# A fused sliding-window attention and feed-forward kernel on one core: residue order 0,2,1,3, VectorE masks for batch 1, w_f copies mostly on ScalarE

## The chip, the core and the metric

The kernel runs on one core of a Trainium2 chip. A core has five engines with a queue each: TensorE (PE in the profile, its weight loads as PEld), VectorE (DVE), ScalarE (ACT), GpSimd (POOL) and SyncE (SP). An engine takes its instructions in the order in which the program holds them and waits on semaphores for the others. Here GpSimd issues the loads that change the type from float32 to bfloat16, SyncE issues the stores and the transposes that a DMA makes. The metric is the device time of one execution in microseconds (us).

## What is computed

For each of 8 batches and 8 heads, 576 positions of 64 numbers attend to earlier positions. Heads 0 to 3 see the last 32 positions; heads 4 to 7 see every fourth position of the last 128. The result, as 4608 tokens of 512 numbers, goes through a gated feed-forward part.

```python
rel = pos[:, None] - pos[None, :]
mask_plain = (rel >= 0) & (rel < 32)
mask_dil = (rel >= 0) & (rel < 128) & (rel % 4 == 0)
scores = np.where(masks, q @ k.T / 8, -1e9)
attn = softmax(scores) @ v
x = attn.transpose(0, 2, 1, 3).reshape(4608, 512)
out = ((x @ w1) * (x @ w2)) @ w3 @ w_out
```

The weights w1 and w2 are 512 by 1024, w3 is 1024 by 1024, w_out is 1024 by 512.

## The kernel before

The kernel multiplies w3 and w_out into one matrix w_f (1024 by 512) on the chip, once, so that a token needs three products: with w1, with w2, and with w_f.

The order of all work is made by a planner that runs while the program is built. Each piece of work is a task with an engine, a supposed duration, dependencies, a priority and a number of PSUM banks (there are eight). `Plan.run` (line 70) plays through a clock of its own, gives each free engine the ready task with the lowest priority number, and hands out banks. The tasks are then emitted in order of their planned starts. So a supposed duration, a rank or a lead changes nothing but the order of the instructions in the queues and the banks.

Attention works by batch. A batch has two halves of heads, u = 0 (plain) and u = 1 (dilated), and in each six blocks of 96 query positions; the dilated heads are sorted by residue of the position modulo 4, so that their window is a band as well. The steps of a batch are:

- load of q, k and v by rows (lines 225 and 234). For batch 0 the first halves of q and k come by SyncE in float32 and ScalarE rounds them (line 240).
- transposition of q, k and v into columns by VectorE: `turn`, lines 344 and 357. v of batches 0 and 1 goes back to rows by TensorE (line 366) and is copied to `vp` (lines 376 and 378). From batch 2 on v is loaded straight into place (lines 248 and 262) with a copy for the halo (line 269).
- scores on TensorE (line 408), a group of blocks at a time, in four banks; exponential on ScalarE (line 419).
- the mask. In batches 0 and 1 (`BIASED = 2`) a group has three blocks, and four products of the identity with a bias table (line 391) put -30000 into the bank before the scores. From batch 2 on a group has five blocks (`GRP`), which may cross batches, and VectorE multiplies the exponentials by 0 or 1 in two halves (line 427). The 0/1 table `mask` is made by GpSimd from the bias table in five operations (line 327).
- P·V on TensorE (line 444), four steps per batch; reciprocal and normalisation on VectorE (lines 455 and 467).
- turning back into columns `XT`: by TensorE (line 484) and a copy by ScalarE or VectorE (lines 492 and 494) in batches 0 and 1, by a DMA transpose that SyncE issues (line 497) from batch 2 on.

The feed-forward part works in units k of 288 tokens, two a batch. For each of eight slices f it makes two groups of four products (line 516, with w1 and with w2), copies the first (ScalarE, line 527) and multiplies it with the second into `gt` (VectorE, line 532). After that eight products with w_f (line 543) give 128 output tokens, copied by ScalarE (line 554) and stored by SyncE (line 565). w_f is made in eight steps: transposes of a slice of w3 (line 573), a copy (ScalarE, line 580), eight products with w_out (line 585) and a copy into `wf_sb` (VectorE, line 595). All 36 outputs need all eight.

At the start, GpSimd's queue holds, in this order: the other loads of batch 0, w1 and w2 by halves of 512 columns, w_out in two halves, six slices of w3, q, k and v of batch 1, two slices of w3, q and k of batch 2, the mask operations, and the loads of v for batch 2. TensorE begins with 12 products on zeros (line 604).

The scores of a batch are held back so that they come `LEAD` batches ahead of the feed-forward part of their batch:

```python
pair = int(16 * (b - LEAD) + 4 * i)
```

Of the kernel before, what the change touches and what calls it, by code (L numbers as in the profile page):

```python
# [10 lines left out]
P = 128  # L11
# [8 lines left out]
S = 576  # L20
# [6 lines left out]
UNIT = 288  # L27
RING = 1152
BIG = 30000.0
BIASED = 2  # L30
TURNED = 2
ORDER = (2, 3, 0, 1)
RANK = dict(E=1.5, VK=1, K=0.4, N=3, T=1.5, VT=0.2, S=0.3, V=0.1, X=0.4)
WARM = 12
W3_FIRST = 6
SHIFT = {}
ON_DVE = ("K0.0", "K0.2", "K0.3", "K1.2", "VK0.1.0", "VK1.0.1")
GRP = 5
WHOLE = ("qn", "kn")
TURN_LAT = 2700  # L40
LEAD = 1.4
# [13 lines left out]
class Plan:  # L55
# [14 lines left out]
    def run(self):  # L70
# [41 lines left out]
        while len(order) < n:  # L112
            progress = True
            while progress:
                progress = False
                for e in engines:
                    if free[e] > now:
                        continue
                    for r, t in sorted(waiting[e], key=lambda x: x[1].prio):
                        if r > now:  # L120
                            continue
                        at = place(t) if t.slot else 0
                        if at is not None:
                            break
                    else:
                        continue
                    waiting[e].remove((r, t))
                    t.start = now
                    if e == "DMA":
                        free[e] = now + t.dur[0]  # L130
                        dma = max(dma, now + t.dur[0]) + t.dur[1]
                        t.end = dma + 1900
                    else:
                        t.end = free[e] = now + t.dur
                        if t.lat == TURN_LAT and dma > now:
                            t.lat += 3300
                    if t.slot:
                        t.place = at
                        held[at : at + t.slot] = [t] * t.slot
                        if t.slot == 4:  # L140
                            kept = None
                    order.append(t)
                    for u in users[id(t)]:
                        left[id(u)] -= 1
                        if not left[id(u)]:
                            r = max(d.end + (0 if d.eng == u.eng else d.lat) for d in u.deps)
                            waiting[u.eng].append((r, u))
                    progress = True
            ahead = [f for f in free.values() if f > now]
            ahead += [r for e in engines for r, _ in waiting[e] if r > now]  # L150
            ahead += [x for x in map(freed, held) if x is not None and x > now]
            if not ahead:
                left = [t.name for t in self.tasks if t.end is None]
                raise RuntimeError(f"the plan does not end: {left[:20]}")
            now = min(ahead)
# [4 lines left out]
def kernel(  # L160
# [28 lines left out]
    w3_pool = ctx.enter_context(tc.tile_pool(name="w3", bufs=8))  # L189
# [63 lines left out]
    def load_v_dil(b, m):  # L253
        vp = vps[b % 2]
        r, mu = 2 * (m // 3), m % 3
        runs = {
            0: [(0, 96, r, 0)],
            1: [(0, 48, r, 96), (48, 48, r + 1, 0)],
            2: [(0, 96, r + 1, 48)],
        }[mu]  # L260
        for p0, n, res, t0 in runs:
            nc.gpsimd.dma_start(  # L262
                out=vp[32 + p0 : 32 + p0 + n, 4:8, m, 0:D],
                in_=v_rows(b, 4, 4 * t0 + res, [[4 * D, n], [S * D, 4], [1, D]]),
            )
# [5 lines left out]
    def load_w(dst, src, c):  # L271
        f = slice(512 * c, 512 * (c + 1))
        nc.gpsimd.dma_start(
            out=dst[:, :, f], in_=src[:, f].rearrange("(a p) f -> p a f", p=P)
        )
# [32 lines left out]
    def blocks():  # L308

        base = bias[:, 6, :]
        by_res = base.rearrange("p (t r) -> p r t", r=4)
        nc.scalar.copy(
            out=bias[:, 0:4, :].rearrange("p i (r t) -> p i r t", r=4),
            in_=by_res.unsqueeze(1).to_broadcast([P, 4, 4, 24]),
        )
        nc.scalar.copy(out=bias[:, 4, :], in_=base)
        nc.scalar.copy(out=bias[:, 5, 0 : QB // 2], in_=base[:, 0 : QB // 2])
# [17 lines left out]
    def turn(b, u, nm, part):  # L337

        src = qk[(nm, b)][:, u, :].bitcast(U32)
        dst, pad = {"qn": (qts, 0), "kn": (kts, PADK), "vn": (vts, PADK)}[nm]  # L340
        d = dst[b % len(dst)].rearrange("p u w c -> p u (w c)").bitcast(U32)[:, u, :]
        if part is None:
# [3 lines left out]
        n, first, odd = ((5, 0, 2 * RUN + 4), (4, 2 * RUN, 5 - 2 * RUN))[part]  # L346
        o = bass.AP(
            tensor=d.tensor,
            offset=d.offset + pad + first,
            ap=[d.ap[0], [1, n], [RUN, 2], [9, 16], [odd, 2]],  # L350
# [3 lines left out]
            offset=src.offset + part * 64,  # L354
            ap=[src.ap[0], [128, n], [32, 2], [1, 32]],
# [200 lines left out]

    def store(i):
        o_sb = held[("o", i)]
        c0, end = i * P, (i + 1) * P
        at = c0  # L560
        while at < end:
            n = min(end, (at // RUN + 1) * RUN) - at
            b, x = at // S, at % S
            row = b * S + 4 * (x % RUN) + x // RUN
            nc.sync.dma_start(
                out=out[row : row + 4 * (n - 1) + 1 : 4, :], in_=o_sb[at - c0 : at - c0 + n, :]
            )
            at += n
# [9 lines left out]
    def w3_keep(ft):  # L578
        w3T[ft] = wk_pool.tile([P, KFF, P], BF16, tag="w3T", bufs=2, name="w3T")
        nc.scalar.copy(out=w3T[ft], in_=held[("x3", ft)])  # L580
# [13 lines left out]
    def w3_done(ft):  # L594
        nc.vector.tensor_copy(out=wf_sb[:, ft, :], in_=held[("wf", ft)])
# [10 lines left out]
    def first_constants():  # L606
        nc.vector.memset(warm, 0.0)
        nc.vector.memset(bias, 0.0)
# [9 lines left out]
    c0 = add("const", "DVE", 2500, [], first_constants, 0)  # L618
    add("warm", "PE", 1840 + 216 * WARM, [c0], warm_up, 0)
# [29 lines left out]

    def loads_w12(c):  # L650
        return [
            load("LW", 800, 3300, [], lambda d=d, s=s: load_w(d, s, c))
# [3 lines left out]
    for i, nm in enumerate(WHOLE):  # L656
        t = add(f"LF{nm}", "SP", 100, [], lambda nm=nm: load_whole(nm, rows_of[nm], 0), -9 + i,
                lat=4100 + 1350 * i)
# [7 lines left out]
    idt = add("ident", "DMA", (600, 0), [], lambda: make_identity(nc, ident), 2.5, lat=-1900)  # L666
    bnd = add("band", "DMA", (700, 0), [c0], band, 2.6, lat=-1800)
    blk = add("blocks", "ACT", 1200, [bnd], blocks, 0, lat=100)
    blk = add("no halo", "DVE", 150, [blk], no_halo, 0, lat=80)
    mk = add("masks", "DMA", (2500, 0), [blk], masks_of_bias, 26.5, lat=-1800)  # L670
    lw12 = [loads_w12(0), loads_w12(1)]
    for c in range(2):
        lwo[c] = load(f"LWO{c}", 600, 3300, [], lambda c=c: load_wo(c))
    def loads_w3(fts):
        for ft in fts:
            lw3[ft] = load(f"LW3.{ft}", 550, 1400, [], lambda ft=ft: load_w3(ft))

    loads_w3(range(W3_FIRST))
    for nm in ("qn", "kn", "vn"):
        loads_rows(nm, 1)  # L680
    loads_w3(range(W3_FIRST, KFF))

    FUSED, w3m = [], []
    for ft in range(KFF):
        x = add(f"W3T{ft}", "PE", 510, [lw3[ft], idt], lambda f=ft: w3_back(f), 6, slot=1,
                after=[w3m[-2] if len(w3m) > 1 else None])
        y = add("W3C", "ACT", 1012, [x], lambda f=ft: w3_keep(f), -1, lat=100,
                after=[w3m[-2] if len(w3m) > 1 else None])
        z = add(f"W3M{ft}", "PE", 1728, [y, lwo[0], lwo[1]], lambda f=ft: w3_mul(f), 7, slot=1)
        w3m.append(z)  # L690
        FUSED.append(add("W3D", "DVE", 688, [z], lambda f=ft: w3_done(f), -1, lat=100))
# [5 lines left out]
    def turns(b, u, nm, pr):  # L697
        parts = (None,) if u == 0 and nm != "qn" else (0, 1)
        old = last_v.get((b - 1, u)) if nm == "vn" else last_s.get((b - 2, u))
        ts = [  # L700
            add(f"T{nm}{b}.{u}.{part or 0}", "DVE",
                1245 if part is None else 750 if part == 0 else 630, [L[(nm, b, u)], c0],
                lambda part=part: turn(b, u, nm, part), pr, lat=80, after=[old])
# [3 lines left out]
        return ts  # L707

    vals, T = {}, {}
    for b in range(B):  # L710
# [4 lines left out]
        for u in range(2):  # L715
            T[(b, u)] = [
                t for nm in ("kn", "qn") for t in turns(b, u, nm, 10 * b + RANK["T"])
            ]
        for u in range(2):
            if b >= 2:  # L720
                break
            tv = turns(b, u, "vn", 10 * b + RANK["T"])
            for half in range(2):
                x = add(f"VT{b}.{u}.{half}", "PE", 420, tv + [idt],
# [8 lines left out]
        if b >= 2:  # L733
            hal = add(f"HALO{b}", "DVE", 820, LV[b], lambda b=b: halo_v(b), 10 * b + 2, lat=80)
# [5 lines left out]
        def group(blocks, biased):  # L740
# [4 lines left out]
            need = [t for at in sorted({x[0:2] for x in blocks}) for t in T[at]]  # L745
# [33 lines left out]
        while steps < 4 * B:  # L779
# [27 lines left out]
            else:  # L807
                x = add("XD" + n, "SP", 100, ns, st.back_dma, 0, lat=TURN_LAT)
# [7 lines left out]
    def ups(k, f):  # L816
# [3 lines left out]
        wl = lw12[f // 4]  # L820
# [14 lines left out]
    def downs(i):  # L835
# [5 lines left out]
        Y[i] = y  # L841
        cy = add("CY", "ACT", 585, [y], lambda: copy_y(i), -1, lat=100,
# [5 lines left out]
    for k in range(2 * B):  # L848
        for f in range(KFF):
            ups(k, f)  # L850
            if f % 3 == 1 and done < n_y and (done + 1) * P <= k * UNIT:
                downs(done)
                done += 1
# [44 lines left out]
```

## Time and profile before

| | us |
|---|---|
| median of five runs (259.69 to 260.49) | 260.34 |
| the profiled execution's own time | 260.24 |
| span in its profile, first to last instruction | 258.5 |
| first up-projection product (line 516) starts | 21.26 |
| last product with w_f ends | 254.1 |

| group in the profile | count | mean ns | busy us |
|---|---|---|---|
| TensorE up-projections, line 516 | 1024 | 286 | 136.0 |
| TensorE products with w_f, line 543 | 259 recorded of 288 | 379 | 65.0 |
| TensorE bias products, line 391 | 32 | 325 | 6.2 |
| VectorE gates, line 532 | 128 | 455 | 57.9 |
| VectorE mask products of five blocks' halves, line 427 | 28 | 650 | 17.5 |
| VectorE copies of w_f, line 595 | 8 | 692 | 5.5 |
| ScalarE exponentials of three blocks, line 419 | 8 | 1129 | 8.8 |
| ScalarE exponentials of five blocks, line 419 | 14 | 1771 | 24.8 |
| ScalarE output copies, line 554 | 36 | 586 | 21.1 |
| GpSimd mask operations, line 327 | 5 | 937 (median) | 4.8 |
| DMA transposes, line 497 | 24 | 4.9 us to landing (median) | |

Matmuls overlap in their pipeline, so the mean of one is longer than the distance from one to the next. A row of the timeline gives the start, the busy time, the engine, the line, what it writes and reads, the shape, the count, and in brackets the idle time before it with what ended it. In a table of stretches each engine has its busy time and, in brackets, its instructions; then come the granted clock of TensorE (1.00 is full), the share of the DMA engines, and GB/s.

### The profile page before, as it was taken

What the parts mean: (1) busy time and instruction counts of PE and PEld (TensorE: products, weight loads), DVE (VectorE), ACT (ScalarE), POOL (GpSimd) and SP (SyncE); (2) the same over time, 40 slices, a digit from 0 to 9 for tenths busy, and PEclk for the clock granted to TensorE, in tenths of its full rate; (3) what the DMA queues carried; (4) which work ended last, traced back from release to release, by engine and by line L of the source; (5) the groups of instructions that cost most, each with busy time, mean ns of one, the idle gap of its engine ahead of it and who ended that gap; (6) DMA issues with size and microseconds to landing.
All of it is one profiled execution on the core that took longest, in us unless ns stands there. A gap on an engine that the chain in (4) does not pass through costs nothing.

```text
span 258.5 us, 6708 instructions
## 1 busy us (share of the span) xinstructions
PE 244.7 (95%) x2699; PEld 167.9 (65%) x2732; DVE 166.5 (64%) x338; ACT 123.1 (48%) x211; POOL 65.2 (25%) x101
## 2 busy tenths in 40 slices
PE   6489999999999999999999999999999999999993
PEld 2367775576577677676667766677766766777661
DVE  3976435979898898898858687666654653333220
ACT  4465464493826373453653535636355343333331
POOL 8612476356401728232033050300000000000000
PEclk9589999999999999999999999999999999999998
DMA  7999999999998999999963949652406162211113
GB/s 221 202 207 202 209 212 210 201 86 190 162 175 159 182 190 116 179 197 206 202 86 53 102 55 144 98 78 53 109 23 93 42 90 63 82 39 44 43 41 122
DMA packets 58030, 33.40 MB, mean 129 GB/s; under 512 B 44688, under 2 KB 47760, under 8 KB 58000
## 3 DMA queue, kind: packets, MB, share of 16 engines
q0 software_dynamic: 37488, 18.81, 56.4%
q1 hardware_dynamic: 20512, 14.16, 25.6%
q8 instruction: 21, 0.34, 0.5%
q14 instruction: 9, 0.07, 0.1%
HBM read 38.80 MB, written 9.44 MB: 187 GB/s over the span
## 4 chain that ended last, share of the span: by engine, by line
PE 91%; ACT 3%; DVE 2%; DMA 2%; issue 1%; ACTq 0%; DVEq 0%
PE ps L516 49%; PE ps L543 23%; PE ps L585 5%; PE ps L444 5%; PE ps L408 4%; ACT et L419 2%; PE ps L391 2%; DMA gt<-in_q_dram 2%; PE ps L573 1%; PE ps L366 1%; PE ps L484 1%; DVE qt L357 1%; DVE kt L344 0%; ACT qn L240 0%; DVE vt L344 0%
## 5 line engine op out<-in xcount | busy, mean ns | idle before, releaser
L516 PE MATMUL ps<-XT,w_sb 128*128 128x288 bf16 x1024 | 136.0, 286 | 0.3 <-DVE gt L532 0.2
L516 PEld LDWEIGHTS <-w_sb 128*128 128x128 bf16 x1024 | 97.7, 98 | 30.1 <-issue 0.6
L532 DVE TENSOR_TENSOR gt<-ps,asb 128x288 bf16<-128x288 f32 x128 | 57.9, 455 | 55.2 <-PE ps L516 53.5
L527 ACT CAST asb<-ps 128x288 bf16<-128x288 f32 x128 | 51.0, 399 | 60.5 <-PE ps L516 57.7
L543 PE MATMUL ps<-wf_sb,gt 128*128 128x512 bf16 x259 | 65.0, 379 | 1.5 <-issue 0.2
L554 ACT COPY osb<-ps 128x512 f32<-128x512 f32 x36 | 21.1, 586 | 52.5 <-PE ps L543 47.1
L543 PEld LDWEIGHTS <-gt 128*128 128x128 bf16 x288 | 28.0, 98 | 27.7
L262 POOL DMA_DIRECT2D vp<-in_v_dram x48 | 30.2, 636 | 48.9 <-PE ps L444 16.2
L419 ACT ACTIVATE et<-ps 128x1920 bf16<-128x1920 f32 (+2 forms) x23 | 34.4, 1506 | 6.1 <-PE ps L408 5.0
L467 DVE TENSOR_TENSOR xo<-ps,rcp 96x384 bf16<-96x384 f32 (+1 forms) x48 | 31.8, 678 | 0.6
L357 DVE STREAM_TRANSPOSE qt<-qn 128x320 uint32<-128x320 uint32 (+1 forms) x32 | 21.6, 674 | 3.4 <-ACT qn L240 3.2
L427 DVE TENSOR_TENSOR et<-et,mask 128x960 bf16<-128x960 bf16 (+1 forms) x30 | 18.1, 630 | 3.8 <-ACT et L419 3.6
L444 PEld LDWEIGHTS <-et 128*128 128x128 bf16 x384 | 14.2, 98 | 3.8 <-ACT et L419 1.3
L444 PE MATMUL ps<-vp,et 128*128 128x65 bf16 x384 | 15.3, 193 | 1.1 <-ACT et L419 1.0
L585 PE MATMUL ps<-wo_sb,w3T 128*128 128x512 bf16 x60 | 14.6, 379 | 0.2
L408 PEld LDWEIGHTS <-kt 32*128 32x128 bf16 x768 | 9.5, 95 | 6.1 <-issue 5.6
L357 DVE STREAM_TRANSPOSE kt<-kn 128x320 uint32<-128x320 uint32 (+1 forms) x16 | 10.9, 683 | 3.6 <-PE ps L408 3.5
L408 PE MATMUL ps<-qt,kt 32*128 32x96 bf16 x768 | 12.9, 206 | 0.0
L344 DVE STREAM_TRANSPOSE kt<-kn 128x576 uint32<-128x576 uint32 x8 | 10.0, 1250 | 2.0 <-PE ps L408 2.0
L580 ACT COPY w3T<-ps 128x1024 bf16<-128x1024 bf16 x8 | 8.1, 1013 | 4.8 <-PE ps L573 4.7
L455 DVE RECIPROCAL rcp<-ps 96x12 f32<-96x12 f32 x32 | 6.5, 214 | 5.3 <-PE ps L444 5.1
L248 POOL DMA_DIRECT2D vp<-in_v_dram x6 | 7.3, 1209 | 10.5 <-PE ps L444 10.3
(49 smaller groups left out, 105.0 us busy)
## 6 DMA issues: line engine op xcount, KB each, us to landing
qn<-in_q_dram POOLq DMA_DIRECT2D x7, 576.0 KB, 7.5
kn<-in_k_dram POOLq DMA_DIRECT2D x7, 576.0 KB, 8.5
w_sb<-in_moe_w_dram POOLq DMA_DIRECT2D x4, 512.0 KB, 12.6
w3n<-in_moe_w_dram POOLq DMA_DIRECT2D x8, 256.0 KB, 15.2
out_dram<-osb SPq DMA_DIRECT2D x8, 256.0 KB, 2.9
out_dram<-osb SPq DMA_DIRECT2D x8, 224.0 KB, 2.9
vp<-in_v_dram POOLq DMA_DIRECT2D x6, 288.0 KB, 10.2
out_dram<-osb SPq DMA_DIRECT2D x8, 192.0 KB, 2.4
```

The source lines that it names most:

```text
L262: nc.gpsimd.dma_start(out=vp[32 + p0 : 32 + p0 + n, 4:8, m, 0:D], in_=v_rows(b, 4, 4 * t0 + res, [[4 * D, n], [S * D, 4], [1, D]]),)
L357: nc.vector.transpose(out=o, in_=i)
L408: nc.tensor.matmul(out=self.sp[:, g, QB * i : QB * i + QB], lhsT=kt[prt, u, QB * m : QB * m + P, c], rhs=qq, start=(c == 0 and not biased) ...
L419: nc.scalar.activation(out=ev, in_=self.sp[:, :, 0:x], func=ACT.Exp, scale=scale)
L444: nc.tensor.matmul(out=self.o[:, g, mm, :], lhsT=grp.et[:, c0 : c0 + P], rhs=vps[self.b % 2][:, 4 * self.u + g, 3 * self.hf + mm, 0 : D + ...
L467: nc.vector.tensor_tensor(out=dst, in0=self.o[0:QB, hs, :, 0:D], in1=self.rcp[0:QB, hs, :].unsqueeze(3).to_broadcast([QB, n, 3, D]), op=AL ...
L516: nc.tensor.matmul(out=o, lhsT=w_sb[:, c, f * P : (f + 1) * P], rhs=unit_cols(k, c), start=(j == 0), stop=(j == DCH - 1),)
L527: nc.scalar.copy(out=a_sb, in_=held[("a", k, f)])
L532: nc.vector.tensor_tensor(out=gt[:, f, c0 : c0 + UNIT].rearrange("p (r m t) -> p m r t", r=2, m=BLK), in0=held[("b", k, f)].rearrange("p ( ...
L543: nc.tensor.matmul(out=y, lhsT=gt[:, f, c0 : c0 + P], rhs=wf_sb[:, f, :], start=(f == 0), stop=(f == KFF - 1),)
L554: nc.scalar.copy(out=o_sb, in_=held[("y", i)])
L585: nc.tensor.matmul(out=o, lhsT=w3T[ft][:, g, :], rhs=wo_sb[:, g, :], start=(g == 0), stop=(g == KFF - 1),)
```

## The change

Parts of it:

- `RES = (0, 2, 1, 3)`: the dilated heads' residues are kept in this order, so that the first three blocks need residues 0 and 2 only. Addresses in `turn`, `load_v_dil`, `store` and the bias table follow. In batch 0, `turn` makes the second half of heads (u = 1) in four parts instead of two, and scores and v's transposes wait only for the parts that their half needs.
- `BIASED = 1`: batch 1's scores are grouped by five with batch 2's and masked by VectorE.
- Three of the eight copies into `wf_sb` stay on VectorE (slices 2, 5 and 7), five go to ScalarE. The `ON_DVE` list of other copies changes as well.
- The first loads have another order: k of batch 1, the first quarter of w1 and of w2, a slice of w3, their second quarters, their second halves, q and v of batch 1, w_out, six slices of w3; after the masks and the first v load of batch 2 the last slice of w3, which waits for one of seven buffers.
- The band of the bias table is built by GpSimd after its second load, with the identity behind it; k's second load comes after both. The memsets are in two tasks, the bias first. The warm-up has 10 products.
- The first up-projections run k = 0 and k = 1 in turn for the first four f, then for the last four.
- The last output is copied in halves by ScalarE and VectorE and stored from two queues (`finish`).
- `RANK` and `LEAD` have other values, and the planner supposes other durations for loads and DMA transposes.

```diff
-BIASED = 2
+BIASED = 1
 TURNED = 2
+DIRECT_V = 2
+RES = (0, 2, 1, 3)
-RANK = dict(E=1.5, VK=1, K=0.4, N=3, T=1.5, VT=0.2, S=0.3, V=0.1, X=0.4)
-WARM = 12
+RANK = dict(E=3, VK=1, K=0.3, N=3, T=0.3, VT=0.1, S=0.3, V=0.2, X=0.3)
+WARM = 10
+FIRST_LOADS = ("k1", "w0", "30", "w1", "w2", "q1", "v1", "o0", "o1", "31", "32", "33", "34", "35", "36", "37")
-ON_DVE = ("K0.0", "K0.2", "K0.3", "K1.2", "VK0.1.0", "VK1.0.1")
+ON_DVE = ("K0.1", "K0.2", "K1.1", "K1.2", "K1.3", "VK0.0.1", "VK1.1.1", "W3D2", "W3D5", "W3D7")
-LEAD = 1.4
+LEAD = 1.1
...
-                        if t.lat == TURN_LAT and dma > now:
-                            t.lat += 3300
+                        if e == "SP" and t.name[0] == "X" and dma > now:
+                            t.end = free[e] = now + t.dur + BUSY
+                            dma += 1.5 * t.dur
...
-    w3_pool = ctx.enter_context(tc.tile_pool(name="w3", bufs=8))
+    w3_pool = ctx.enter_context(tc.tile_pool(name="w3", bufs=7))
...
-        nc.scalar.copy(
-            out=bias[:, 0:4, :].rearrange("p i (r t) -> p i r t", r=4),
-            in_=by_res.unsqueeze(1).to_broadcast([P, 4, 4, 24]),
-        )
+        for low in range(2):
+            nc.scalar.copy(
+                out=bias[:, 0:4, 48 * low : 48 * low + 48].rearrange("p i (h t) -> p i h t", h=2),
+                in_=by_res[:, low, :, :].unsqueeze(1).to_broadcast([P, 4, 2, 24]),
+            )
...
+    def finish(i):
+        o_sb = wk_pool.tile([P, d_model], F32, tag="osb", bufs=3, name="osb")
...
+        nc.scalar.copy(out=o_sb[:, lo], in_=held[("y", i)][:, lo])
+        nc.vector.tensor_copy(out=o_sb[:, hi], in_=held[("y", i)][:, hi])
+        nc.scalar.dma_start(out=rows[:, lo], in_=o_sb[:, lo])
+        nc.sync.dma_start(out=rows[:, hi], in_=o_sb[:, hi])
...
+    def w3_done(ft, eng):
+        if eng == "ACT":
+            nc.scalar.copy(out=wf_sb[:, ft, :], in_=held[("wf", ft)])
+        else:
+            nc.vector.tensor_copy(out=wf_sb[:, ft, :], in_=held[("wf", ft)])
...
+    c1 = add("const", "DVE", 1200, [], first_constants, -99)
+    c0 = add("const2", "DVE", 1400, [c1], constants, -98)
+    add("warm", "PE", 1840 + 216 * WARM, [c1], warm_up, 0)
...
+    WC = (slice(0, 256), slice(256, 512), slice(512, 1024))
...
-    bnd = add("band", "DMA", (700, 0), [c0], band, 2.6, lat=-1800)
-    blk = add("blocks", "ACT", 1200, [bnd], blocks, 0, lat=100)
+    bnd = add("band", "DMA", (800, 0), [c1], band, 1.5, lat=150)
+    blk = add("blocks", "ACT", 1200, [bnd], blocks, -5, lat=100)
...
+        if ft + 7 in lw3:
+            lw3[ft + 7].after.append(x)
+            lw3[ft + 7].deps.append(x)
...
-        parts = (None,) if u == 0 and nm != "qn" else (0, 1)
+        if u == 0:
+            parts = (None,) if nm != "qn" else (0, 1)
+        else:
+            parts = (2, 3, 4, 5) if b == 0 else (0, 1)
...
-                x = add("XD" + n, "SP", 100, ns, st.back_dma, 0, lat=TURN_LAT)
+                x = add("XD" + n, "SP", 1300, ns, st.back_dma, 0, lat=1200)
...
-    for k in range(2 * B):
-        for f in range(KFF):
-            ups(k, f)
-            if f % 3 == 1 and done < n_y and (done + 1) * P <= k * UNIT:
-                downs(done)
-                done += 1
+    half = KFF // 2
+    begin = [(k, f + h) for h in (0, half) for k in range(2) for f in range(half)]
+    for k, f in begin + [(k, f) for k in range(2, 2 * B) for f in range(KFF)]:
+        ups(k, f)
+        if k > 1 and f % 3 == 1 and (done + 1) * P <= k * UNIT:
+            downs(done)
+            done += 1
```

## The prediction

> **What bounds the kernel now.** I read the granted clock and span first (0.983, 258.5 us), then the busy totals, the 40 slices, a table of chosen stretches, the chain of waits, and the timeline of the stretches where TensorE isn't full.
>
> ```profile
> PE 244.7 (95%) x2699; PEld 167.9 (65%) x2732; DVE 166.5 (64%) x338; ACT 123.1 (48%) x211; POOL 65.2 (25%) x101
> PE   6489999999999999999999999999999999999993
> PEclk9589999999999999999999999999999999999998
> 10.00:23.00 13.00, 11.72 (x221) 8.54 (x220) 10.38 (x21) 7.82 (x10) 3.30 (x7) 0.83 1.22 204
> 34.00:48.00 14.00, 13.89 (x103) 8.12 (x103) 7.54 (x12) 6.81 (x8) 9.56 (x13) 1.00 1.11 211
> 48.00:65.00 17.00, 16.42 (x274) 11.43 (x278) 15.16 (x29) 10.91 (x14) 8.47 (x13) 1.00 1.31 150
> 65.00:80.00 15.00, 14.73 (x209) 10.15 (x216) 13.22 (x26) 8.38 (x13) 2.67 (x4) 1.00 1.23 170
> ```
>
> TensorE is full from 21.3 to 254.1 us. From there the end moves only if TensorE gets less work, starts its stream of up-projections (UP below, line 516) earlier, or waits longer. In the stretches (first pair of numbers: length and TensorE busy) it idles 0.11 of 14, 0.58 of 17 and 0.27 of 15 us: some 0.9 us up to 72 us. So a TensorE instruction removed there is worth its whole duration, and work moved between VectorE and ScalarE is worth nothing by itself.
>
> **The opening.** Here VectorE is the one to watch.
>
> ```profile
> 6.04 1.40 DVE L357 STREAM_TRANSPOSE qt<-qn 128x320 uint32<-128x320 uint32 x2 [3.24 <-ACT qn L240]
> 7.39 1.26 DVE L344 STREAM_TRANSPOSE kt<-kn 128x576 uint32<-128x576 uint32 x1
> 9.79 1.46 PE L366 MATMUL ps<-ident,vt 128*128 128x128 bf16 x12 [4.38 <-DVE vt L344]
> 12.14 0.67 PE L408 MATMUL ps<-qt,kt 32*128 32x96 bf16 x24
> 15.07 0.23 DVE L455 RECIPROCAL rcp<-ps 96x12 f32<-96x12 f32 x1 [1.42 <-PE ps L444]
> 21.26 1.63 PE L516 MATMUL ps<-XT,w_sb 128*128 128x288 bf16 x12
> ```
>
> k's first half is turned at 8.65, but TensorE's queue has v's transposes ahead of the scores, and bias lacks its halo until 10.4, so scores start at 12.1. In the changed order bias and scores come first, the band is built before k's second load is issued, and scores can start at about 8.7. That doesn't start UP 3.4 us earlier, because UP waits for the last of three normalised pieces, and VectorE then works without a pause. Adding its rows: the four turns of head half 0 end at 9.57 as before. Half 1 of q, k and v now comes in quarters. The rows with 256 and 576 elements (0.62 and 1.25 us) give 2.0 ns per element and 0.12 fixed, so 0.44 and 0.37 per quarter, 4.86 for twelve (4.08 for six before). One v copy 0.94, four reciprocals 0.92, two wide norms 1.90, three narrow ones 1.65, batch 1's k turn, which now stands here, 1.25, two XT copies 0.90. End: 22.0; neighbouring turns overlap by some 0.15 us, so I take **21.9, or +0.6 us**. Before, the same engine had 2.3 us of waits in this stretch; those are used up by the splitting and the k turn. Bounds: 20.6 (if all overlap as well) and 23.5 (each hand-over to ScalarE late). The shorter warm-up (10 for 12), the split memsets and ScalarE's four bias copies (some 1.1 us, ahead of q's arrival at 4.83) lie beside the loads: nothing. k's second load is issued about 1 us later, behind the band, but two loads are landing until 9.5, so it still lands near 10.9. If the copies ran past 4.86, each microsecond would delay everything.
>
> Eight transposes of w3 (row: 0.45 us) move into TensorE's idle time there: **-0.45**, if w3's first slice has landed. Loads land in their order at about 205 GB/s (the two w_out halves, 0.52 MB each, landed at 25.1 and 27.7). From 12.2 us on k of batch 1 (0.59 MB), two quarters of w1/w2 (0.26 each) and this slice (0.26) come: 18.9 us, needed at about 20.4. Were it late, the last X transposes, behind it in TensorE's queue, and UP with them would be late by the same.
>
> **Batch 1's masks.** Before:
>
> ```profile
> 48.77 0.65 PE L391 MATMUL ps<-bias,ident 128*128 128x288 bf16 x4
> 49.73 0.66 PE L391 MATMUL ps<-bias,ident 128*128 128x288 bf16 x4
> 51.02 0.65 PE L391 MATMUL ps<-bias,ident 128*128 128x288 bf16 x4 [0.26 <-ACT et L419]
> 52.05 0.65 PE L391 MATMUL ps<-bias,ident 128*128 128x288 bf16 x4
> ```
>
> In the chain these four cost 0.49 to 0.66 us, 2.45 in all. The score products stay as many: **-2.45**. The waits of that time (the 0.9 above) belong to the old order: **-0.9**. ScalarE: four exponentials of 1.13 go, two of 1.77 come and one grows from 0.82 to about 1.45: nothing. VectorE: four mask products of 0.65 come and two grow from 0.35 to 0.55, 3.0 in all; five w_f copies of 0.69 leave it for ScalarE (about 0.59 there, by the same-sized output copy). ScalarE is 49 to 64% busy there, so these hide; if its queue fell behind, w3's transposed slices, copied by the same engine, would reach TensorE late, by up to 0.59 for each copy ahead.
>
> The mask is a new wait. GpSimd builds it from 35.3 on, in five operations of which the first two take 1.18 and 0.70 and the next two 0.94 each; until now nothing wanted it before 67 us. Batch 1's first mask product wants the first two at some 37.5 us. GpSimd's loads ahead of it each wait for the eighth before: in the trace q of batch 1, at 25.40, waited for the first w_out half, with seven loads between. By that rhythm k of batch 2 is issued when the second w_out half has landed. Up to it pass 0.59 (k) + 2.10 (w1, w2) + 0.26 (w3) + 1.18 (q, v) + 1.05 (w_out) = 5.18 MB, 25.3 us, so at 37.5; issue 0.71, two mask operations 1.88: mask at 40.2, two products, first P·V at 41.6. TensorE's own work up to it (UP of batch 0, two score groups, v) brings it there 1.1 us earlier. Behind the waiting product VectorE holds a v copy, one gate and the second group's products; their masks are there at 42.1. Later the X transposes wait some 0.5 for three norms: **+1.65** for these. Ends: 0.6, if loads run 2% faster, and 4, if 512-byte rows (the quartered w1/w2) slow the queue. I take the value near the row, because 1 KB and 2 KB rows moved at the same rate.
>
> **A rule against it.** Between 4.2 and 7.6 us TensorE was busy 1.2 us, 37%, and the granted clock fell to 0.5 at 7.5, two microseconds after the last warm-up product; it rose again at 14.4. The Trainium skill (TensorE: Matmul & The Clock Gate, Part 1, "What's actually happening") wants at least one idle window of 3.4 us for the drop. The changed opening has no gap over 2.6 us, so by the rule UP starts at full clock: 0. By the row, a window that is only about 40% busy may drop it, and 17.8 to 21.2 holds two P·V of 0.37, a w3 step of 0.45 and two X steps of 0.26, if one of each pair falls outside it about 1.35 us; UP would then run to 24.6 at half clock: +1.4. I take 0, as the gaps of 0.76 and 0.42 us after 15 us cost no clock in this trace, and keep 1.4 for a rival.
>
> **The rest.** LEAD 1.4 to 1.1 and the new ranks place scores later. By the built order, batch 3's last needed DMA transpose has some 11 us between its P·V and its first UP; norms take about 2.5 and the transpose 4.9 (median; maximum 7.8): covered by 3.7, and where the cover is gone each excess microsecond is lost. RES, the reordered first UPs (k = 0 and 1 alternate by half f) and w3's seven buffers: nothing, since RES changes addresses only and the last w3 slice, now issued after the masks and a v load, lands near 57 and is wanted near 62; the first half f needs the w1/w2 quarters at 21.9 to 25, which land by 21.6, and the last half lands at 26.7, needed at 29.8. The last copy (0.59) is shared by two engines, by its rate some 0.35 each, two queues: **-0.3**.
>
> **Sum:** +0.64 - 0.45 - 2.45 - 0.9 + 1.65 - 0.3 = -1.8. The profiled execution took 260.24 (258.5 span and 1.7 around it), 0.1 below the median of five, 260.34: **258.5 us**.
>
> **Rivals.**
> - *Opening better than counted* (UP at 20.9, mask not awaited): 257.1. For it: 2.3 us of VectorE waits go. Against: quarters and k turn fill them. 0.13.
> - *Cold stream:* UP starts at half clock, 258.5 + 1.4 = 259.9. For it: the 37% row. Against: the rule. 0.17.
> - *Late masks, the slower side:* GpSimd's queue runs 4 us behind, so the mask is at 44.2; VectorE stands at the product with gates behind it, TensorE stands at P·V. From 2 us late on the saving is gone; at 4 us: 262.5. For it: a four-deep chain load, issue, mask, product with 0 slack. Against: first-in first-out landing held within 0.3 us. 0.15.
> - *Late transposes:* one microsecond lost in each of batches 2 to 5, 262.5 at the worst, 261 likely. For it: lead cut. Against: 3.7 us cover. 0.10.
> - That the bias products don't go is excluded: 16 fewer stand in the built order.
>
> **Chances.** Forecast 0.45 (257.8 to 259.4). Within 0.2% (0.5 us) is what a measurement here can't tell from no change. Faster: 0.45 + 0.13 + 0.05 of the cold case = 0.63; same: 0.08 of it and 0.02 of the late ones, 0.10; slower 0.27. The range 256.9 to 261.3 leaves the far ends of the late cases and little below.
>
> **What would show it.** Right: UP's first product at about 21.9, no line of 16 bias products after 40 us, one wait of VectorE for the mask of 1 to 3 us near 40 with TensorE idle about 1 us, granted clock 1.0 from 15 us. Wrong: the clock at 0.5 in 21 to 25 us, the mask after 42, UP waiting for XT from the DMA transposes after 90 us, or UP before 21.

## The result

The changed kernel took 259.08 us (median of 20 executions, 258.41 to 261.54) against 259.96 before (median of 39). By the means, 259.45 and, without one execution at 265.59, 260.01, the ratio is 0.9978, 95% interval 0.9964 to 0.9993: some 0.6 us faster. The forecast was 1.8 us, so the direction was right and the size was not. The profiled execution (258.74, span 256.9) is 1.5 us below the profiled one before, much nearer to the forecast than the ratio is. Most of what follows is about this difference.

The executions fall into two groups. Of the 20, fifteen took 258.4 to 259.7 us (the lower group; median 258.86, mean 258.95) and five 260.6 to 261.5 (the upper group; mean 260.95). Before, 20 of the 38 took 259.5 to 260.0 and 18 took 260.1 to 260.7; the profiled execution of before, 260.24, is one of the upper ones.

### The profile page after: what moved, and what is told of

It is laid out like the page before. It is cut to its first block, busy times and chain, and to the rows that moved or that the text cites. A ratio compares the mean times of both kernels' runs of the same rounds, so it can differ in the third digit from the quotient of the medians.

```text
span 256.9 us, 6672 instructions
## 1 busy us (share of the span) xinstructions
PE 242.8 (95%) x2685; PEld 166.7 (65%) x2714; DVE 167.3 (65%) x345; ACT 123.4 (48%) x214; POOL 66.5 (26%) x103
## 4 chain that ended last, share of the span: by engine, by line
PE 86%; DVE 2%; issue 1%; POOL 1%; ACT 0%; ACTq 0%; DVEq 0%
PE ps L525 48%; PE ps L552 24%; PE ps L606 5%; PE ps L453 4%; PE ps L417 3%; PE ps L594 1%; DVE et L436 1%; PE ps L493 0%; DVE vt L351 0%; DVE qt L366 0%; POOL mask L333 0%; DVE gt L541 0%; POOL kn L231 0%; DVE osb L574 0%; ACT osb L573 0%
## 5 line engine op out<-in xcount | busy, mean ns | idle before, releaser
L563 ACT COPY osb<-ps 128x512 f32<-128x512 f32 x35 | 20.5, 586 | 56.4 <-PE ps L552 55.0
L268 POOL DMA_DIRECT2D vp<-in_v_dram x48 | 29.8, 630 | 41.6 <-PE ps L453 20.3
L476 DVE TENSOR_TENSOR xo<-ps,rcp 96x384 bf16<-96x384 f32 (+1 forms) x48 | 31.2, 676 | 0.4
L436 DVE TENSOR_TENSOR et<-et,mask 128x960 bf16<-128x960 bf16 (+1 forms) x34 | 22.0, 670 | 9.1 <-ACT et L428 7.9
L366 DVE STREAM_TRANSPOSE qt<-qn 128x320 uint32<-128x320 uint32 (+3 forms) x34 | 22.4, 668 | 1.9 <-ACT qn L246 1.7
L366 DVE STREAM_TRANSPOSE kt<-kn 128x320 uint32<-128x320 uint32 (+3 forms) x18 | 11.6, 644 | 3.5 <-PE ps L417 3.4
L231 POOL DMA_DIRECT2D kn<-in_k_dram x8 | 5.5, 693 | 29.4 <-DVE kt L366 24.2
L606 PEld LDWEIGHTS <-w3T 128*128 128x128 bf16 x64 | 6.0, 98 | 6.2
```

The source lines that it names most:

```text
L268: nc.gpsimd.dma_start(out=vp[32 + p0 : 32 + p0 + n, 4:8, m, 0:D], in_=v_rows(b, 4, 4 * t0 + res, [[4 * D, n], [S * D, 4], [1, D]]),)
L366: nc.vector.transpose(out=o, in_=i)
L436: nc.vector.tensor_tensor(out=ev, in0=ev, in1=mk, op=AL.mult)
L476: nc.vector.tensor_tensor(out=dst, in0=self.o[0:QB, hs, :, 0:D], in1=self.rcp[0:QB, hs, :].unsqueeze(3).to_broadcast([QB, n, 3, D]), op=AL ...
L606: nc.tensor.matmul(out=o, lhsT=w3T[ft][:, g, :], rhs=wo_sb[:, g, :], start=(g == 0), stop=(g == KFF - 1),)
```

## The profile after

The busy totals, the TensorE slices and the granted clock:

```profile
PE 242.8 (95%) x2685; PEld 166.7 (65%) x2714; DVE 167.3 (65%) x345; ACT 123.4 (48%) x214; POOL 66.5 (26%) x103
PE   7678997999999999999999999999999999999993
PEclk9899999999999999999999999999999999999999
```

TensorE has 1.9 us less work and is as full as before from the fourth slice on. The table of stretches, with the same edges as before:

```profile
10.00:23.00 13.00, 9.86 (x182) 7.88 (x171) 11.92 (x28) 7.75 (x11) 5.51 (x9) 0.87 1.28 203
34.00:48.00 14.00, 12.02 (x205) 8.64 (x206) 12.34 (x22) 9.84 (x13) 10.60 (x13) 1.00 1.14 210
48.00:65.00 17.00, 16.95 (x207) 10.82 (x207) 9.84 (x17) 10.49 (x15) 9.08 (x14) 1.00 1.28 165
65.00:80.00 15.00, 14.90 (x163) 9.66 (x164) 12.80 (x24) 6.25 (x12) 2.76 (x5) 1.00 1.11 152
```

The idle time has moved: 34 to 48 us now holds 1.98 us (0.11 before), 48 to 65 holds 0.05 (0.58 before). The timeline of the opening:

```profile
8.71 0.44 PE L417 MATMUL ps<-qt,kt 32*128 32x96 bf16 x24 [1.76 <-DVE kt L351]
19.84 0.61 PE L594 MATMUL ps<-ident,w3n 128*128 128x128 bf16 x8
21.56 1.14 PE L525 MATMUL ps<-XT,w_sb 128*128 128x288 bf16 x8 [0.79 <-DVE XT L503]
```

Scores start at 8.7 us and the up-projections (UP) at 21.56, 0.3 later than before. And the new wait:

```profile
38.07 0.72 POOL L231 DMA_DIRECT2D kn<-in_k_dram  x1 [1.87 <-DVE gt L541]
38.82 4.97 POOL L333 TENSOR_SCALAR mask<-bias 128x384 bf16<-128x384 bf16 x5
40.72 2.05 DVE L436 TENSOR_TENSOR et<-et,mask 128x960 bf16<-128x960 bf16 x2 [1.03 <-POOL mask L333]
41.86 0.36 PE L453 MATMUL ps<-vp,et 128*128 128x65 bf16 x6 [0.91 <-DVE et L436]
42.83 0.35 PE L453 MATMUL ps<-vp,et 128*128 128x65 bf16 x6 [0.62 <-DVE et L436]
```

The k load of batch 2 is issued at 38.07, GpSimd makes the mask behind it, VectorE waits 1.03 us for it, and P·V on TensorE waits 0.91 and 0.62 us. Two mask products took 2.05 us here, where a pair takes 1.3 elsewhere; GpSimd was writing further masks beside them, but no run shows whether that is the reason.

## The experiments

All times are us. A number ahead of a bracket is a median, the bracket holds the lowest and the highest execution, and "ratio" is against the kernel before, with its interval. A clock given for a whole execution is the mean granted clock of TensorE.

**The changed kernel again, unedited.**

> The changed kernel once more, unedited, for the spread of its executions. Of its 20 executions 15 took 258.4 to 259.7 us and five 260.6 to 261.5. Theory (clock phase): the clock gate's window runs free of the program, and in some executions a cold window reaches into the dense stream of up-projections after 21.6 us; then the executions fall into two groups about 2 us apart, the slow group mostly with a mean granted clock near 0.985 instead of 0.991. Rival (late masks): a jitter of the loads moves the mask operations, so that the times spread evenly and without regard to the clock.

258.99 (258.3 to 261.76), ratio 0.9973 (0.9945 to 1.0001). Eight at 258.3 to 259.1 with clocks of 0.991 to 0.999; four at 260.7 to 261.8 with 0.983 to 0.987. Two groups, as the theory has it. In the first 20 executions the clock separates them less well: it is 0.985 to 0.987 in four of the lower group and 0.993 in one of the upper. The 29 executions of the kernel before in this series split cleanly: twelve at 259.5 to 259.9 with 0.989 to 0.993, seventeen at 260.1 to 260.7 with 0.983 to 0.985.

**Masks early.** GpSimd's mask operations directly behind the w_out loads; TensorE's order stays.

```diff
-mk = add("masks", "DMA", (2500, 0), [blk], masks_of_bias, 26.5, lat=150)
+mk = add("masks", "DMA", (2500, 0), [blk], masks_of_bias, 16.5, lat=150)
```

> GpSimd's five mask operations stand right behind the w_out loads instead of behind the k load of batch 2; TensorE's order is unchanged. The profile of the changed kernel shows TensorE waiting 0.91 and 0.62 us for the first mask products, 1.03 us of VectorE's wait being for the mask. Theory (clock phase): the mask wait is a fixed cost; without it every execution is about 1 us shorter (fast group near 257.7) and the slow group stays, 2 us above. Rival (late masks cause the slow group): the slow group goes and the fast group gains about 1 us.

256.96 (256.85 to 259.56), ratio 0.9899 (0.9866 to 0.9932). The timelines of GpSimd and TensorE:

```profile
19.83 4.76 POOL L333 TENSOR_SCALAR mask<-bias 128x384 bf16<-128x384 bf16 x5
40.71 0.53 PE L453 MATMUL ps<-vp,et 128*128 128x65 bf16 x12
```

P·V no longer waits (40.71, no bracket). The gain over the changed kernel's lower group of the same series (median 258.62, here 256.9) is 1.7, the 1.53 of waiting and a little more. Two of six executions stayed 1.3 and 2.7 higher, so late masks don't make all of the scatter. The same kernel again:

> The kernel with early masks again, for its interval: fast group near 256.9, and by either theory of a clock window a quarter to a third of the executions 1.5 to 2.7 us above it.

257.0 (256.73 to 258.8), ratio 0.9891 (0.9867 to 0.9914); one of six 1.8 higher. So three of twelve executions are raised although TensorE doesn't wait for the masks. No profile caught one of them.

**25 warm-up products for 10.**

> 25 warm-up products on zeros instead of 10, to fill TensorE's idle time up to the first scores at 8.7 us. Theory (clock phase): the clock stays up over the opening more often and the slow group becomes rarer, but it needn't vanish, because TensorE is only about two thirds busy from 15 to 21.6 us; fast group unchanged near 258.7 (the warm-up ends at about 8.6 us). Rival (late masks): same two groups in the same share as in the unedited kernel.

259.16, ratio 0.9976 (0.9953 to 1.0). Eight at 258.5 to 259.3 with clocks of 0.997 to 1.0, four at 260.7 to 261.0 with 0.992 or 0.993. The opening is now at full clock, which changes no time, and the upper group stands out alone: 0.007 of 257 us is 1.8 us of full clock lost, or 3.6 us at half clock. This is the clearest sign that the upper group has lost clock.

**TensorE kept busy before the stream.** Products on zeros into unused columns; the first filling behind steps VT0.1.0, X0.1 and X0.2, the second ahead of the instructions that TensorE waits before.

```diff
-WARM = 10
+WARM = 25
...
+    FILL = {"S0.3.0": ("VT0.1.0", 12), "V0.3": ("X0.1", 10), "A0.0": ("X0.2", 10)}
...
+        for _ in range(n):
+            nc.tensor.matmul(
+                out=ps[:, at[name], 384:512], lhsT=warm[:, 0:P], rhs=warm[:, 0:P], start=True, stop=True
+            )
```

> The changed kernel with TensorE kept busy to the first up-projection: 25 warm-up products, and 14, 12 and 12 products of 128 columns of zeros (0.056 us each at full clock) behind the first v transposes of head half 1, the second and the third X step, where TensorE idled 0.9, 0.8 and 0.8 us. They write columns that no step uses; all else keeps its order. Theory (clock phase): no cold window is left to reach into the stream, so all executions fall into the fast group, 258.4 to 259.3 us, and none is near 261. Rival (late masks or another jitter): a quarter to a third of the executions stays at 260.6 to 261.7.

> The filling again, with its products (12, 10, 10) set ahead of the instruction that TensorE waits before, so that they don't delay the copies of the steps whose banks they use; in the first filled kernel the stream started at 22.98 instead of 21.56 us. Theory (clock phase): all executions in the fast group, now at its lower end, 258.3 to 259.0 us, stream from about 21.6 us. Rival: the first filling lost its slow group only because its stream started later, hidden by the mask wait; then a group near 261 comes back.

First: 259.4 (258.55 to 259.52), ratio 0.9973 (0.9963 to 0.9984). Second: 258.64 (258.5 to 259.2), ratio 0.9954 (0.9937 to 0.9971). None of 17 is above 259.6. In the first, though, eight of eleven stand at 259.34 to 259.52, above the range that was expected. And the second expectation was wrong on the start of the stream, so that the two runs can't tell the theory from its rival: in both the stream starts late. The second one's timeline:

```profile
22.95 1.14 PE L525 MATMUL ps<-XT,w_sb 128*128 128x288 bf16 x8
42.18 0.79 PE L453 MATMUL ps<-vp,et 128*128 128x65 bf16 x12
```

The filling waits too, for the copies from its banks, and delays the stream by 1.4 us, to 22.95; yet the time is that of the changed kernel's lower group, because P·V at 42.18 then finds its mask ready. **In this kernel 1.4 us lost at the head of the stream cost nothing: the mask wait gave it back.**

**Filling and early masks together.**

> The same filling and the mask operations early, as in the run with early masks. Theory: both effects add: all executions near 256.9, some 1.7 us below the filled kernel and 3.3 below the kernel before. Rival: filling changes nothing, executions again in two groups near 256.9 and 259.5.

> The second filling with the mask operations early. Theory: all executions near 256.9 us, 3 us below the kernel before; it is the fastest of the series and has no second group. Rival: a second group near 259.5 stays, or the start of the stream moves again and the gain over the filled kernel stays near 0.6 us.

258.77, ratio 0.9952 (0.9936 to 0.9969), and 258.73 (257.43 to 259.07), ratio 0.994 (0.9916 to 0.9963). Both expectations failed: with no mask wait behind it, the later start of the stream (23.05 and 23.29 in the profiles) is paid in full. Early masks alone stay the best version.

**The w3 transposes behind the first eight up-projections** (25 warm-up products).

> The kernel with 25 warm-up products, with its first w3 transposes (0.45 us of TensorE) and their copy moved behind the first eight up-projections, so that the time from 17 to 21.5 us is emptier. Theory (clock phase): the slow group grows from a third to a half or more of the executions, at mean clocks 0.006 to 0.008 below the fast ones, and a profile of it shows the clock at 0.5 for 3.4 us after 21 us; the fast group is at most 0.5 us above 258.6. Rival: the share stays a third.

258.72 (258.43 to 259.13), ratio 0.9955 (0.9937 to 0.9972). No execution in the upper group, where the theory of a cold head wanted more of them. The theory's guess failed, though with six executions only: at a share of one in four, none in six has a chance of 18%. This step also brings TensorE to the masks 0.45 us later.

**More profiles, for an execution that lost its clock.** The last two runs also gave ten timed executions.

> The changed kernel once more, for one more profile. Theory: with a chance of about 3 in 10 it is one of the slow group, with the clock at 0.5 within 21 to 26 us; else it repeats the profile at hand.

> One more profile of the changed kernel. If it is a slow execution (near 261): theory (cold window at the head of the stream): granted clock 0.5 for 3.4 us somewhere in 20 to 27 us, and all after it as in the fast profile. Rival (cold window at the mask wait): clock 0.5 for 3.4 us in 41 to 47 us. Rival (not the clock): clock 1.0 throughout, and TensorE waiting longer for the masks or for XT.

> One profile of the kernel with 25 warm-up products, whose slow executions (4 of 12, near 260.9) have a mean clock 0.007 below the fast ones. Same three answers as for the look at the changed kernel.

> The same once more, for the chance of a slow execution: a cold window of 3.4 us either in 20 to 27 or in 41 to 47 us, or none.

> One more profile of the kernel with 25 warm-up products. If slow (near 260.9): theory: granted clock 0.5 for 3.4 us somewhere in 20 to 27 us. If fast again, the place of the cold window stays unseen.

> One more profile of the changed kernel. If slow (near 261): theory: granted clock 0.5 for 3.4 us within 20 to 27 us, beside the cold window of the opening. If fast, it repeats the profile at hand.

The first five profiles repeated the lower group (258.5 to 258.6), one of them at a mean clock of 0.987. Of the ten timed executions one, 260.88, was of the upper group. The last profile, 259.45 at a mean clock of 0.980, has a cold head: the clock is at one half where the stream of up-projections begins. Each row has the stretch, its length, TensorE's busy time and products, then the clock:

```profile
18.50:21.91 3.41, 1.94 (x40) 1.00 1.36 202
21.91:25.32 3.41, 3.11 (x18) 0.50 1.25 210
25.38:34.00 8.62, 8.62 (x72) 1.00 1.15 209
```

and from its timeline

```profile
22.21 2.08 PE L525 MATMUL ps<-XT,w_sb 128*128 128x288 bf16 x8 [0.79 <-DVE XT L503]
42.93 0.34 PE L453 MATMUL ps<-vp,et 128*128 128x65 bf16 x6
```

The clock fell at 21.91, after a stretch in which TensorE was busy 57% and had no pause above 0.9 us, and came back 3.4 us later. The first eight up-projections took 2.08 instead of 1.14. That lost 1.6 us, and the opening had lost 0.65; but P·V at 42.93 doesn't wait for its mask, its second part only 0.29 us, and the execution ends only 0.7 us above the profile at hand. So a cold head is real, and this one didn't make an execution of the upper group: the mask wait swallows most of it. In the kernel with early masks nothing would swallow it; a cold head of 1.6 us would fit its raised executions, but none was caught.

What makes the upper group, then? A candidate is the stretch around the mask wait, first in the changed kernel, then in the second filled one:

```profile
40.00:43.40 3.40, 1.88 (x26) 1.00 1.12 210
43.40:46.80 3.40, 3.35 (x53) 1.00 1.12 214
```

```profile
40.00:43.40 3.40, 3.28 (x40) 1.00 1.11 209
43.40:46.80 3.40, 3.40 (x55) 1.00 1.12 212
```

In the changed kernel 3.4 us around the mask wait are busy 1.88, about the share after which the clock fell above. If a window lay so and the clock fell behind it, the next 3.4 us would run at half clock, and nothing later would give the 1.7 us back, as TensorE is full from there on.

But such a share doesn't decide it. Within a trace the clock changes only at multiples of 3.41 us from one another (in the profile with the cold head at 8.25, 15.08, 21.91 and 25.32), and from one trace to the next these moments lie elsewhere. Two of these windows that were as empty, each with the one behind it: the head of the stream in the changed kernel's second run, and the mask wait in its first profile (whose clock fell at 10.32, nine windows before 41.04):

```profile
18.75:22.16 3.41, 1.94 (x32) 1.00 1.35 203
22.16:25.57 3.41, 3.41 (x35) 1.00 1.24 208
```

```profile
41.04:44.45 3.41, 1.92 (x18) 1.00 1.12 210
44.45:47.86 3.41, 3.35 (x54) 1.00 1.10 211
```

With the same 1.94 us busy the clock fell in one execution and held in another, and at the mask wait it held. So the busy share alone doesn't tell when the clock falls.

For the mask wait as the place speak the size (the upper groups lie 1.8 to 2.5 above their lower ones; half clock in one window costs 1.7), the mean clock 0.007 lower with 25 warm-up products, and where the group occurs: of the executions of the changed kernel and of the one with 25 warm-up products 14 of 58 lie above 260.5, of the kernels that come to the masks later (both fillings, the one below with the old tail, the w3 step moved) none of 35. Against it: 29 of these 35 also have their opening filled, so the later arrival isn't tested by itself, and three of twelve executions with early masks are raised without any such wait. No profile caught an execution of the upper group. That it lost clock is likely; where it lost it stays open.

**The masks alone, put into the kernel before.**

```diff
-BIASED = 2
+BIASED = 1
```

> The kernel before with one part of the change alone: BIASED = 1. The planner reorders all that follows. 16 bias products (2.45 us of the chain, with some 0.5 us of waits) go and VectorE's masks come, with the mask table ready at 40 us, ten microseconds before it is wanted. Theory (TensorE is the bound): 2 to 2.5 us shorter than before, near 257.8 if the planner's other moves cost nothing. Rival (VectorE takes its place as the bound between 50 and 110 us, where it is 85 to 89% busy): no gain or a loss, with TensorE waiting for gates or normalised pieces.

259.04, ratio 0.9958 (0.9943 to 0.9973): about 1.2 us, half of what the removed products are worth. The profiled execution, 260.15, is the slowest of the twelve. It has a stall that the kernel before doesn't have (19.84 of these 20 us busy there):

```profile
80.00:100.00 20.00, 17.33 (x220) 11.05 (x217) 17.89 (x34) 8.61 (x14) 9.12 (x14) 1.00 1.40 159
```

and in the list of its waits (who waits, for what; us in total, how many times, the longest)

```profile
PE ps L516 <- DMA XT<-xo: 1.3, 1, 1.3
PE ps L516 <- ACT et L419: 1.3, 1, 1.3
```

2.67 us are lost there, for a DMA transpose and for an exponential, by this list not for VectorE as the rival had it. The planner's new order is the likely reason; how much of the stall the faster executions have isn't known. In the changed kernel this stretch is full (19.84 of 20).

**Bias products put back into the filled kernel** (`BIASED = 2`).

> The filled kernel with batch 1 masked by bias products again (BIASED = 2); the planner reorders what follows the first 104 up-projections. The difference to the filled kernel is what VectorE's masking of batch 1 is worth inside this change. My sum: 2.45 us of products come back, about 1.6 us of waits for the masks go, so 0.5 to 1.3 us slower than the filled kernel. Rival (the masks are a gain of the full 2.5 us): 2.5 slower. Rival (nothing gained): the same.

261.97, ratio 1.0073 (1.0054 to 1.0091), against 259.4 for the filled kernel: 2.6 slower, 2.4 between the profiled executions. From the start of the stream to the last product with w_f TensorE is busy 229.85 us here and 227.56 in the filled kernel, 2.3 more, and idles about the same (2.15 and 1.98). That is the rival's full price; the filled kernel's profile has no mask wait that could be saved. The planner's new order is part of this difference as well.

**The old tail in the filled kernel.**

```diff
-        if i == n_y - 1:
+        if i == n_y:
```

> The filled kernel with the last output copied by ScalarE alone and stored from one queue, as before. My sum: 0.3 us slower than the filled kernel. Rival: the two copies run one after the other, so that nothing is gained.

259.53, ratio 0.9978 (0.9966 to 0.999); 0.1 above the filled kernel's 259.4 by the medians, 0.3 by the means, inside the intervals. The traces are finer. The last copies before, in this run, and in the changed kernel:

```profile
254.10 0.59 ACT L554 COPY osb<-ps 128x512 f32<-128x512 f32 x1 [1.14 <-PE ps L543]
```

```profile
253.39 0.58 ACT L563 COPY osb<-ps 128x512 f32<-128x512 f32 x1 [1.14 <-PE ps L552]
```

```profile
252.76 0.37 ACT L573 COPY osb<-ps 128x256 f32<-128x256 f32 x1 [1.14 <-PE ps L552]
253.17 0.42 DVE L574 COPY osb<-ps 128x256 f32<-128x256 f32 x1 [5.10 <-ACT osb L573]
```

VectorE starts only when ScalarE has finished: 0.37 and 0.42 one after the other, where one copy took 0.59. The second half is ready 0.24 later than the whole was. But from the start of the last copy to the end of the span are 4.37 us before, 4.34 in this run and 4.17 in the changed kernel: the smaller stores from two queues give back more than that, and some 0.2 is gained.

## Why the forecast was wrong

- **Opening, forecast +0.6:** UP began at 21.56 instead of 21.9, so +0.3. VectorE was the bound as said; only 0.54 us of its waits were left behind the norms, ahead of the first XT copy.
- **w3 step into idle time, -0.45:** there, at 19.84.
- **Bias products, -2.45:** right; 2.3 to 2.6 when put back where no wait hides it.
- **Waits of the old order, -0.9:** of TensorE's idle time up to 72 us some 0.25 stayed beside the new waits, so about -0.65.
- **Mask wait, +1.65:** mechanism right, mask and P·V within 0.6 us of the forecast. TensorE waited 0.30 for an exponential and 1.53 for the masks, 1.8; the 0.5 for norms didn't come. Taking the masks out of the way gave 1.7.
- **Transposes by DMA, VectorE load, ScalarE load: nothing,** and nothing was seen: TensorE is busy at least 19.79 of every 20 us from 80 to 240.
- **Tail, -0.3:** the copies don't run at the same time; the smaller stores still gave 0.2.
- **Clock, taken as 0 with 1.4 kept for a rival: this step failed.** I weighed the rule of the Trainium skill (TensorE: Matmul & The Clock Gate, "What's actually happening": one idle window of 3.4 us before the clock falls) against the row of this trace (a fall after a window busy 37%) and took the rule. The run above shows a fall after a window busy 57% with no pause over 0.9 us. The measurement decides: here a half-busy window can be enough, though the clock held after others just as empty. The length of a cold window, 3.4 us, agrees with the page. I had also counted the window ahead of UP as emptier than it is: 1.35 us of work (the steps listed give 1.08 if one of each pair falls outside), where 1.94 was measured. And I expected the loss at the head of the stream; there most of it is hidden by the mask wait. What the term of 0 left out is the upper group: five of 20 executions, 2.0 us above the others, with a mean clock 0.007 lower in the kernel with 25 warm-up products, where the opening doesn't blur it. Where in the execution the clock is lost stays open.

For the profiled execution the sum held: 258.5 said, 258.74 came. In part that is luck: the opening came out 0.3 better than its term, and TensorE's waits up to 72 us 0.4 worse (from 0.90 to 2.08 us, so +1.2, where -0.9 and +1.65 make +0.75).

The measured difference of the means is smaller for three reasons. The execution of before that I summed against, 260.24, lies 0.23 above the mean of its kind, 260.01. The lower group of the changed kernel has its mean, 258.95, 0.45 above the forecast, 0.24 of it in the profile. And the five of the upper group add 0.50 to the mean. From 1.74 (260.24 - 258.5) these take 1.18 and leave the measured 0.56. The first reason is the clock once more, as far as the groups of before go with it: the execution that I summed against had 0.983, and 12 of the 29 in the series above 0.989 to 0.993. Its trace has the half clock from 7.58 to 14.41, two windows, where the first profile of the changed kernel has one; that the faster executions of before had one as well is inferred. The price in the rival of the cold stream, 259.9 for its executions, was 1 too low for the upper group, if that is what it meant, and 0.4 too high for the cold head that was seen.

## What to carry to other kernels

When a wait is set by an operation in a queue that has no need to stand so late, as the masks behind the k load here, move the operation before tuning anything else: with this one number moved the changed kernel is 1.0 to 1.1% faster than the kernel before, without it 0.2%. A loss ahead of a wait is hidden by it, so two repairs don't add: filling the opening, which came with a later start of the stream, went without the upper group while the masks were late, and cost 1.8 us once they were early. And when executions fall into groups, find out first which group the profile that you reckon from belongs to: here that alone was 0.2 of the 1.2 us by which the forecast was too high. Whether a wait also costs clock behind it, by emptying a window, is a question that this case leaves open.

## What was not expected of the hardware

The clock fell to 0.5 after a window of 3.41 us in which TensorE was busy 1.94 us, and held in another execution after a window with the same 1.94. It came back after windows busy 90% or more (0.90, 0.91, 0.93 and 0.98 in four profiles, full in others) and stayed low for a second window after 86%, 78%, 75% and 35%; so the cold part of the opening is 3.4 us long in some executions and 6.8 in others. Filling waits as the real products do: products on zeros set into idle time waited 0.6 to 0.9 us for the copies from their banks and delayed the stream by 1.4 us. A copy of one half of a PSUM bank by VectorE started only after ScalarE's copy of the other half (0.37, then 0.42 us), by a wait in the program; whether the hardware needs it isn't shown.
